# Block 3's layernorm moved to the first step of the second MLP chunk, its turning moved ahead of one weight step, and two w1 buffers exchanged

## The chip, the core and the metric

The kernel runs on one core of a Trainium2 chip. The metric is the device time of one launch in microseconds (us). The core has a matrix engine (TensorE, "PE" in the profile, with its weight loads as "PEld"), a vector engine (VectorE, "DVE"), a scalar engine (ScalarE, "ACT"), a general engine (GpSimd, "POOL") and a queue engine (SyncE, "SP"). Each takes its instructions in the order in which they were written. They wait for each other by semaphores. Transfers are issued here from SP's queue and from POOL's.

## The reference

x is 2048 rows of 640 numbers. Each row is layernormed; the result goes through a Fourier layer and through an MLP, and both are added to x:

```python
xn = _layernorm(x, axis=-1)
a = einsum("bsd,ed->bse", xn, dft_hid_re)      # wr
b = einsum("bsd,ed->bse", xn, dft_hid_im)      # wi
y = einsum("ts,bse->bte", dft_seq_re, a) - einsum("ts,bse->bte", dft_seq_im, b)
h = gelu(einsum("bsd,df->bsf", xn, w1) + b1)   # w1 is 640 x 1536
out = x + y + einsum("bsf,fd->bsd", h, w2) + b2
```

Everything is float32. A product is made of three matmuls, since each operand is split in a rounded part and a rest (`split`: ScalarE copies the rounded part, VectorE subtracts it from the source).

## The kernel before, in words

The MLP takes the 2048 rows in four chunks t of 512. The first two are done in full; the last two share products by sums and differences of operands (the letters a11, s1, ob and so on in `form_of`, and the w1 sums in `sums_w1`). After the MLP come the products of the Fourier layer, which fill the rest of the program.

The change lies in the second chunk (t = 1), in the branch `elif i < NF - 2` of the main loop. One pass of it, unit i = 0 to 9, is for the PE fifteen matmuls of `hidden(g + 2)` (the first MLP product, two units ahead, g = 12 + i) and fifteen of `output(g)` (the second). What `hidden` leaves in a PSUM bank, `gelu(g + 2)` turns into a pair `hs`: ScalarE applies gelu and copies the rounded part, VectorE subtracts the rest. `output(g)` reads the pair that was made two units before. The pairs are called here by their g: pair 18 is made in unit 4 and read in unit 6, pair 19 is made in unit 5 and read in unit 7.

Behind these, each unit writes side work to the same queues, in this order: `second_block(i)`, then `prep_w(k)` by the table `w_early`.

- Rows 12 to 15 (128 rows each) are block 3, the fourth chunk's rows in their natural order: `ln_stats`, `ln_scale` and `ln_apply` normalize them on VectorE (one square root on ScalarE), and 16 transfers, L203, write them to the DRAM tensor `xs`. `load_z(t)` reads a chunk back as the tile z, four transfers on SP, and `turn_z2` / `turn_z1` transpose z on VectorE (lines L786 and L792). z2 is the third chunk, z3 the fourth. The tile z, the tile xo and the later wz share one buffer, `zo`.
- `prep_w(0)` to `prep_w(5)` prepare two of the five column blocks j of wr and wi, three steps for each. Step 0 and 3 transpose both (L396, out of `wraw`) and issue the loads of the next block; every step splits its pieces into the staging tile `wst` and has POOL write them to the DRAM tensor `wit` (L418). The first step of a block writes two pieces, the second two, the third three. `wst` holds two of the wide pieces, so a step's ScalarE copy waits until the step before has landed in `wit`. That wait also holds up whatever ScalarE and VectorE have queued behind, the next gelu among it.
- From unit 7 on `sums_w1` and `split_w1` make the sums of w1 in a tile `rq` and split them into the tiles TW[0], TW[1], ... (pool "twp", tags tw0 and tw1). That pool takes the place of the pool of `wst`, `wraw` and `wt` when `open_tw` runs.

After unit 9 come the last two outputs, `head(0)`, `mid(0)`, `head(1)` and `finish(0)`: the products of the shared chunks. Between them stand the second chunk's five closing blocks, e = 0 to 4 (`outs`): ScalarE adds the bias in PSUM (L368), VectorE transposes the bank (L371), POOL adds it to xo (L373). `forms_ob` stands among them: one add of 1024 columns (L452), the split of TW[1], and the split of the form ob. `head(1)` starts in the bank of block e = 2, then in that of e = 3; the first product of `finish(0)` goes on in a bank that a VectorE add of `mid(0)` (L452, `banks<-banks,fifth`) reads.

No scheduler reorders this: the order in the queues is the order in which the code writes it.

Of the kernel before, what the change touches and what calls it, by code (L numbers as in the profile page):

```python
# [11 lines left out]
F32R = mybir.dt.float32r  # L12
# [3 lines left out]
P = 128  # L16
# [10 lines left out]
def kernel(  # L27
# [57 lines left out]
    def pool(name, side="left", stack=ctx):  # L85
        return stack.enter_context(tc.tile_pool(name=name, bufs=1, side=side, reuse_waits="tile"))
# [93 lines left out]
    def ln_stats(c):  # L180
        m = MV
        st = ST[c % 2]
        half = D // 2
        for h in range(2):
            nc.vector.bn_stats(st[:, h, :], xt[c][:, h * half : (h + 1) * half])
        nc.vector.bn_aggr(m[:, c % 4, 0:2], st.rearrange("p a b -> p (a b)"))
# [12 lines left out]
    def ln_apply(c, queue=nc.sync):  # L199
        m = MV[:, c % 4]  # L200
        nc.vector.tensor_scalar(xt[c], xt[c], m[:, 0:1], m[:, 3:4], op0=ALU.subtract, op1=ALU.mult)
        for k in range(NC):
            queue.dma_start(xs[c % NC * NC + k, c // NC * B : (c // NC + 1) * B], xt[c][k * B : (k + 1) * B])  # L203
# [25 lines left out]
    def load_z(t):  # L229
        z = out_pool.tile([P, NB, DQ], F32, tag="zo", bufs=1, name=f"z{t}")  # L230
        Z["z"] = z
        for q in range(Q):
            v = xs[:, t * B : (t + 1) * B, q * DQ : (q + 1) * DQ].rearrange("n r d -> r n d")
            nc.sync.dma_start(z[q * B : (q + 1) * B], v)
# [124 lines left out]
    def load_xo(t):  # L359

        xo[t] = out_pool.tile([P, NB, DQ], F32, tag="zo", bufs=1, name=f"xo{t}")
        for q in range(Q):
            nc.sync.dma_start(xo[t][q * B : (q + 1) * B], rows_of(x, t)[:, :, q * DQ : (q + 1) * DQ])
# [12 lines left out]
    A = {}  # L376
# [43 lines left out]
    def prep_w(s):  # L420

        j, k = divmod(s, 3)
        if j >= ND:
            return
        if k == 0:
            turn_w(0, j)
            turn_w(1, j)
            if j + 1 < ND and j != WEARLY - 1:
                load_w(0, j + 1)
                load_w(1, j + 1)  # L430
        (r1, r2, r4), (i1, i2, i4) = (
            (A["wt", m][:, : 2 * P], A["wt", m][:, 2 * P : 4 * P], A["wt", m][:, 4 * P :]) for m in range(2)
        )
# [12 lines left out]
        if k == 2:  # L446
            put_w(3, j, r1)
            put_w(4, j, i1)
            put_w(5, j, r2)
# [325 lines left out]
    TW, RQ = {}, {}  # L775
    parks = {}

    def form_of(name, cc, src, dst):
        FX[name, cc] = dst
        split(dst[:, 0], dst[:, 1], src)  # L780

    def lane(tag, k):
        return whole[tag][:, k * 2 * TB : (k + 1) * 2 * TB].rearrange("p (a b) -> p a b", a=2)
# [7 lines left out]
    def turn_z1(dst, j):  # L791
        nc.vector.transpose(dst.rearrange("p (n i) -> p n i", i=B), Z["z"][:, :, j * B : (j + 1) * B])  # L792

    def two(lo):
        return A["zs"][:, lo * TB : (lo + 2) * TB].rearrange("p (a b) -> p a b", a=2)

    def load_rq(q):
        if q >= NF // 2:
            return
        RQ[q] = A["xf"].tile([P, 4, 2 * P], F32, tag="rq", bufs=1, name=f"rq{q}")  # L800
        v = w1.rearrange("(q c i) f -> q i c f", q=Q, i=B)
        for k in range(Q):
            nc.sync.dma_start(RQ[q][k * B : (k + 1) * B], v[k, :, :4, 2 * q * P : 2 * (q + 1) * P])

    def sums_w1(q):
# [6 lines left out]
        add(r[:, 2:4, P:], r[:, 2:4, P:], r[:, 0:2, :P], ALU.subtract)  # L812
        add(r[:, 2:4, :P], r[:, 2:4, :P], r[:, 2:4, P:], ALU.subtract)

    def split_w1(q):
        if q >= NF // 2:
            return
        TW[q] = A["tw"].tile([P, 2, 8 * P], F32R, tag=f"tw{q % 2}", bufs=1, name=f"tw{q}")
        split(TW[q][:, 0], TW[q][:, 1], RQ.pop(q).rearrange("p a b -> p (a b)"))
        TW[q] = TW[q].rearrange("p a (c f) -> p a c f", c=4)  # L820

# [148 lines left out]
    def open_tw():  # L970
        A["es"].close()
        A["w"] = None
        A["es"] = ExitStack()
        A["tw"] = pool("twp", stack=A["es"])

    def open_xf():
        es_rows.close()
        A["esx"] = ExitStack()
        A["xf"] = pool("xfp", side="right", stack=A["esx"])
        A["xfx"] = A["xf"].tile([P, 2, 2, TB], F32R, name="xfx")  # L980
        A["fifth"] = A["xf"].tile([P, TB], F32, name="fifth")
        load_rq(0)

    def second_block(i):

        if i == 0:
            load_z(2)
            ln_stats(12)
            ln_stats(13)
        if i == 1:  # L990
            ln_stats(14)
            ln_stats(15)
        if i == 2:
            ln_scale(12, 4)
            for c in range(12, 16):
                ln_apply(c, nc.gpsimd if c < 14 else nc.sync)
        if i == 3:
            A["zs"] = place("xc01", (P, 30 * P), F32, name="zs")
            turn_z2(two(0), 0)
            turn_z2(two(2), 2)  # L1000
            turn_z1(ZT[:, 0], 4)
            load_z(3)
        if i == 4:
            form_of("a11", 0, two(0)[:, 0], lane("as", 5))
            open_xf()
        if i == 5:
            form_of("a11", 1, two(0)[:, 1], lane("xc23", 0))
            form_of("oa", 0, ZT[:, 0], lane("xc23", 1))
        if i == 6:
            form_of("a12", 0, two(2)[:, 0], lane("xc23", 2))  # L1010
            turn_z2(ZT, 2)
            turn_z2(two(4), 0)
            turn_z1(A["zs"][:, 6 * TB : 7 * TB], 4)
            load_xo(1)
            open_tw()
        if i == 7:
            sums_w1(0)
            split_w1(0)
            load_rq(1)
            form_of("a22", 0, ZT[:, 0], lane("r01", 0))  # L1020
        if i == 8:
            form_of("a22", 1, ZT[:, 1], lane("r01", 1))
            add(ZT, ZT, two(4))
        if i == 9:
            form_of("s1", 0, ZT[:, 0], lane("r01", 2))
            form_of("s1", 1, ZT[:, 1], lane("r01", 3))
            add(two(4), two(0), two(4), ALU.subtract)
            add(ZT, ZT, two(0), ALU.subtract)
# [18 lines left out]
        form_of("s4", 0, two(2)[:, 0], XTT[:, 3])  # L1047
        form_of("s4", 1, two(2)[:, 1], XTT[:, 4])

    w_early = {0: (0,), 1: (1,), 2: (2,), 3: (3,), 4: (4,), 5: (5,)}  # L1050
    prep_w1(3)
    gelu(1, acc1)
    for g in range(NG):
        t, i = divmod(g, NF)
        if t == 0:
            if i:
                prep_w1(i + 3)
            prep_w2(i + 1)
            load_w1(i + 6)
            load_w2(i + 4)  # L1060
            if i != 8:
                first_block(i)
            if i == NF - 1:
                open_w()
                acc = hidden(g + 2)
                output(g)

                def fill(k):
                    for e in ((0,), (1, 2))[k]:
                        add_block(xo[0], e, oacc[0][e], f"ot0_{e}", bias=b2c[:, e : e + 1])  # L1070

                gelu(g + 2, acc, fill)
                outs(0, (3, 4))
            elif i == NF - 2:
                output(g)
                gelu(g + 2, hidden(g + 2))
            else:
                acc = hidden(g + 2) if g else acc2
                if i == NF - 3:
                    for j in range(ND):  # L1080
                        prep_xt(1, j)
                        if j + 2 < ND:
                            transpose_z(1, j + 2)
                gelu(g + 2, acc)
                if i == 8:
                    first_block(i)
                if i == 9:
                    ln_stats(10)
                    ln_stats(11)
                output(g)  # L1090
        elif i < NF - 2:
            acc = hidden(g + 2)
            gelu(g + 2, acc)
            output(g)
            second_block(i)
            for k in w_early.get(i, ()):
                prep_w(k)
        elif i == NF - 2:
            output(g)
            forms_s2()  # L1100
            head(0)
            forms_s3()
        else:
            output(g)
# [36 lines left out]
        outs_at((3, 4), (0, 1), done=True)  # L1141

    outs(1, (0,), yt=lambda n: AB[:, 0], done=False)
    forms_ob()
    outs_at((2, 1), (4, 5))
    mid(0, rest)
    forms_s4()
    head(1)
# [657 lines left out]
```

## Time and profile before

| | us |
|---|---|
| median of 3 runs | 850.76 |
| lowest and highest | 850.23, 850.90 |
| the profiled execution's own time | 853.42 |
| its span, first to last instruction | 851.6 |
| PE busy in the span | 842.5 |
| VectorE, ScalarE, GpSimd busy | 668.0, 355.3, 53.6 |

The profile is of one execution. A row of the timeline gives the start from the beginning of the span, the duration (of all merged instructions), the engine, the line, the operation, the tiles out<-in, the shape and the count; in square brackets stands how long the engine had been idle and what ended that. A matmul of 512 columns stays in the array for 0.39 us, but the next one starts 0.227 us behind it, so PE rows overlap, and a lost moment shows as a start that comes late.

### The profile page before, as it was taken

How to read it: one execution, taken by the hardware profiler on the slowest of the kernel's cores; microseconds unless marked ns; L12 is line 12 of the kernel's file. 1: busy time of each engine (PE TensorE's matmuls, PEld its weight loads, DVE VectorE, ACT ScalarE, POOL GpSimd, SP SyncE). 2: the span in 40 equal slices, each digit the busy share in tenths (PEclk: the TensorE clock that was granted, in tenths of full speed). 3: DMA queues.
4: the chain of work that ended last, by engine and by line, in shares of the span. 5: the costliest groups of instructions: out<-in, count | busy, mean ns of one | idle time of the engine just before them, and what ended most of it. 6: DMA issues, size and time to landing. Idle time of an engine off the chain costs nothing.

```text
span 851.6 us, 10345 instructions
## 1 busy us (share of the span) xinstructions
PE 842.5 (99%) x3707; PEld 694.5 (82%) x3707; DVE 668.0 (78%) x841; ACT 355.3 (42%) x499; POOL 53.6 (6%) x78
## 2 busy tenths in 40 slices
PE   8999999999999999999999999999999999999997
PEld 6888888778888888888888888888888888888886
DVE  6766764795757888879988787899977898885687
ACT  7454533555655554333434343232322423223241
POOL 0000313131221300000000000000000000000001
PEclk9999999999999999999999999999999999999999
DMA  6667799738669998948743669763865879805464
GB/s 185 187 185 186 162 215 252 196 79 195 207 216 347 360 218 158 188 102 204 164 137 95 177 211 285 171 139 97 213 164 171 253 184 228 312 18 179 124 170 108
DMA packets 207363, 158.45 MB, mean 186 GB/s; under 512 B 81040, under 2 KB 180880, under 8 KB 206800
## 3 DMA queue, kind: packets, MB, share of 16 engines
q1 hardware_dynamic: 198368, 134.59, 62.2%
q0 software_dynamic: 4400, 21.89, 6.5%
q10 hardware_dynamic: 4544, 1.31, 0.6%
q8 instruction: 29, 0.48, 0.2%
q14 instruction: 22, 0.18, 0.1%
HBM read 114.76 MB, written 42.99 MB: 185 GB/s over the span
## 4 chain that ended last, share of the span: by engine, by line
PE 83%; DVE 4%; DMA 4%; ACT 3%; issue 3%; SPq 2%; POOL 1%; ACTq 0%; POOLq 0%; DVEq 0%
PE banks L278 27%; PE banks L279 26%; PE banks L280 26%; PE banks L304 3%; DMA x<-in_A_x_dram 1%; DMA wit<-wst 1%; SPq L388 1%; DMA xs<-x 1%; ACT ab L322 1%; SPq L203 0%; SPq L178 0%; POOL wit L418 0%; DVE r L161 0%; ACT hs L326 0%; DVE tw L161 0%
## 5 line engine op out<-in xcount | busy, mean ns | idle before, releaser
L278 PE MATMUL banks<-as,xab 128*128 128x512 f32 x411 | 160.0, 389 | 0.6 <-DVE zs L371 0.6
L279 PE MATMUL banks<-as,xab 128*128 128x512 f32 x411 | 159.9, 389 | 0.0
L280 PE MATMUL banks<-as,xab 128*128 128x512 f32 x411 | 159.9, 389 | 0.0
L160 ACT ACTIVATE as<-r 128x1024 fp32r<-128x1024 f32 x80 | 85.0, 1062 | 177.9 <-PE banks L280 149.5
L161 DVE TENSOR_TENSOR as<-r,as 128x1024 fp32r<-128x1024 f32 x80 | 97.1, 1215 | 41.5 <-ACT as L160 41.5
L278 PEld LDWEIGHTS banks<-as,xab 128*128 128x128 f32 x411 | 77.2, 188 | 17.0 <-DVE zs L371 1.0
L279 PEld LDWEIGHTS banks<-as,xab 128*128 128x128 f32 x411 | 77.2, 188 | 16.0
L280 PEld LDWEIGHTS banks<-as,xab 128*128 128x128 f32 x411 | 77.2, 188 | 15.9
L278 PE MATMUL banks<-as,xc 128*128 128x512 f32 x224 | 87.1, 389 | 0.0
L279 PE MATMUL banks<-as,xc 128*128 128x512 f32 x224 | 87.1, 389 | 0.0
L280 PE MATMUL banks<-as,xc 128*128 128x512 f32 x224 | 87.1, 389 | 0.0
L160 ACT ACTIVATE as<-rt 128x1024 fp32r<-128x1024 f32 x32 | 34.0, 1063 | 70.5 <-PE banks L280 62.5
L304 PE MATMUL banks<-xtt,xab 128*128 128x512 f32 x240 | 57.2, 391 | 0.2 <-ACT xtt L160 0.2
L304 PEld LDWEIGHTS banks<-xtt,xab 128*128 128x128 f32 x240 | 44.7, 188 | 10.1 <-ACT xtt L160 0.6
L278 PEld LDWEIGHTS banks<-as,xc 128*128 128x128 f32 x224 | 42.1, 188 | 8.8
L280 PEld LDWEIGHTS banks<-as,xc 128*128 128x128 f32 x224 | 42.1, 188 | 8.7
L279 PEld LDWEIGHTS banks<-as,xc 128*128 128x128 f32 x224 | 42.0, 188 | 8.7
L161 DVE TENSOR_TENSOR as<-rt,as 128x1024 fp32r<-128x1024 f32 x32 | 38.8, 1211 | 5.3 <-ACT as L160 5.3
L160 ACT ACTIVATE as<-u 128x1024 fp32r<-128x1024 f32 (+1 forms) x24 | 22.1, 919 | 48.2 <-PE banks L280 48.2
L512 DVE STREAM_TRANSPOSE r<-raw 128x1024 f32<-128x1024 f32 x32 | 39.5, 1239 | 3.0 <-PE banks L280 2.4
L161 DVE TENSOR_TENSOR as<-u,as 128x1024 fp32r<-128x1024 f32 (+1 forms) x24 | 24.9, 1041 | 18.8 <-ACT as L160 18.8
L512 DVE STREAM_TRANSPOSE rt<-raw 128x1024 f32<-128x1024 f32 x32 | 38.8, 1229 | 0.9 <-PE banks L280 0.8
(353 smaller groups left out, 1622.9 us busy)
## 6 DMA issues: line engine op xcount, KB each, us to landing
raw<-in_A_dft_seq_re_dram SPq DMA_DIRECT2D x64, 256.0 KB, 5.5
raw<-in_A_dft_seq_im_dram SPq DMA_DIRECT2D x64, 256.0 KB, 5.1
ws<-wit SPq DMA_DIRECT2D x15, 384.0 KB, 5.8
xo<-in_A_x_dram SPq DMA_DIRECT2D x16, 320.0 KB, 5.9
xab<-wit SPq DMA_DIRECT2D x13, 384.0 KB, 4.0
wit<-wstp POOLq DMA_DIRECT2D x12, 384.0 KB, 3.7
x<-in_A_x_dram SPq DMA_DIRECT2D x14, 320.0 KB, 4.4
xs<-x SPq DMA_DIRECT2D x56, 80.0 KB, 1.8
```

The lines of the kernel that those rows point to most:

```text
L160: nc.scalar.activation(h, s, AF.Copy)
L161: nc.vector.tensor_tensor(l, s, h.bitcast(F32), op=ALU.subtract)
L278: nc.tensor.matmul(acc, wh, mh, start=first, stop=False, skip_group_check=goes_on)
L279: nc.tensor.matmul(acc, wh, ml, start=False, stop=False, skip_group_check=goes_on)
L280: nc.tensor.matmul(acc, wl, mh, start=False, stop=last, skip_group_check=goes_on)
L304: nc.tensor.matmul(acc, W1[i][:, a, j * P : (j + 1) * P], XT[j][:, b], start=n == 0, stop=n == len(steps) - 1)
L322: nc.scalar.activation(a, acc, AF.Gelu_apprx_tanh, bias=b1c[:, i : i + 1])
L388: nc.sync.dma_start(t[q * B : (q + 1) * B], v[:, :, s0 : s0 + B])
L512: nc.vector.transpose(held(pieces[g][2], u).rearrange("p c (n i) -> p c n i", i=B), r.rearrange("p n (c i) -> p c n i", i=B))
```

## The change

Six edits, all in the order of the side work:

1. `ln_stats`, `ln_scale` and `ln_apply` of rows 12 to 15 are all written in unit 0, ahead of `prep_w(0)`, instead of in units 0, 1 and 2. The writes of rows 12 and 13 thereby stand ahead of all of `prep_w` in POOL's queue, and those of rows 14 and 15 ahead of `load_z(2)` in SP's.
2. `prep_w(3)`, `(4)` and `(5)` move from units 3, 4, 5 to units 4, 5, 6.
3. z3 is turned in unit 5, behind the forms of that unit and ahead of `prep_w(4)`, instead of in unit 6 behind `prep_w(5)`. `load_xo(1)`, which needs z3's buffer, moves with it.
4. `load_rq(0)` is written in unit 5 instead of unit 4.
5. TW[1] is allocated at `open_tw`, ahead of TW[0], so that TW[0] gets the upper and TW[1] the lower place, the one in which `wst` lay.
6. Of the closing blocks, e = 2 is written ahead of `forms_ob`, and e = 1 stays behind it.

```diff
     def split_w1(q):
         if q >= NF // 2:
             return
-        TW[q] = A["tw"].tile([P, 2, 8 * P], F32R, tag=f"tw{q % 2}", bufs=1, name=f"tw{q}")
+        if q != 1:
+            new_tw(q)
...
         A["tw"] = pool("twp", stack=A["es"])
+        new_tw(1)
...
         A["fifth"] = A["xf"].tile([P, TB], F32, name="fifth")
-        load_rq(0)
...
         if i == 0:
-            load_z(2)
-            ln_stats(12)
-            ln_stats(13)
-        if i == 1:
-            ln_stats(14)
-            ln_stats(15)
-        if i == 2:
+            for c in range(12, 16):
+                ln_stats(c)
             ln_scale(12, 4)
             for c in range(12, 16):
                 ln_apply(c, nc.gpsimd if c < 14 else nc.sync)
+            load_z(2)
...
-        if i == 6:
-            form_of("a12", 0, two(2)[:, 0], lane("xc23", 2))
             turn_z2(ZT, 2)
             turn_z2(two(4), 0)
             turn_z1(A["zs"][:, 6 * TB : 7 * TB], 4)
+            load_rq(0)
             load_xo(1)
+        if i == 6:
+            form_of("a12", 0, two(2)[:, 0], lane("xc23", 2))
+            prep_w(5)
             open_tw()
...
-    w_early = {0: (0,), 1: (1,), 2: (2,), 3: (3,), 4: (4,), 5: (5,)}
+    w_early = {0: 0, 1: 1, 2: 2, 4: 3, 5: 4}
...
     outs(1, (0,), yt=lambda n: AB[:, 0], done=False)
+    outs_at((2,), (4,))
     forms_ob()
-    outs_at((2, 1), (4, 5))
+    outs_at((1,), (5,))
```

VectorE around z3. In the names, `hs` is a gelu pair, `wst<-wt_1` a split of the second column block of wr (1217, 1258) or wi (1219, 1260), `zt/zs<-z_1212` the turning of z3, `xc<-zs` and `xc<-zt` the splits of forms. Before, from pair 19 on:

```order
L328 TENSOR_TENSOR hs<-ab,hs 128x512
L161 TENSOR_TENSOR xc_127<-zs,xc_127 128x512
L161 TENSOR_TENSOR xc_127<-zt,xc_127 128x512
L161 TENSOR_TENSOR wst<-wt_1_1217,wst 128x256
L161 TENSOR_TENSOR wst<-wt_1_1219,wst 128x256
L161 TENSOR_TENSOR wst<-wt_1_1217,wst 128x256
L328 TENSOR_TENSOR hs<-ab,hs 128x512
L161 TENSOR_TENSOR xc_127<-zs,xc_127 128x512
L786 STREAM_TRANSPOSE zt<-z_1212 128x1024
L786 STREAM_TRANSPOSE zs<-z_1212 128x1024
L792 STREAM_TRANSPOSE zs<-z_1212 128x512
L328 TENSOR_TENSOR hs<-ab,hs 128x512
```

and now, from pair 19 on as well:

```order
L328 TENSOR_TENSOR hs<-ab,hs 128x512
L161 TENSOR_TENSOR xc_127<-zs,xc_127 128x512
L161 TENSOR_TENSOR xc_127<-zt,xc_127 128x512
L786 STREAM_TRANSPOSE zt<-z_1212 128x1024
L786 STREAM_TRANSPOSE zs<-z_1212 128x1024
L792 STREAM_TRANSPOSE zs<-z_1212 128x512
L161 TENSOR_TENSOR wst<-wt_1_1260,wst 128x256
L417 SCALAR_TENSOR_TENSOR wst<-wt_1_1260,wst 128x128
L452 TENSOR_TENSOR wt_1_1260<-wt_1_1260,wt_1_1258 128x256
L161 TENSOR_TENSOR wst<-wt_1_1260,wst 128x256
```

Behind pair 19 stood the last step of the block; now the turning of z3 stands there, and then the block's middle step, so two steps of wr and wi come behind it.

SP's queue in the same units. `wraw0_1` and `wraw1_1` are the loads of the second column block, `xs<-x14, x15` the writes of block 3's rows, `ys` the stores that free the buffer `zo` for z2. Before:

```order
L930 DMA ys2_62<-xo0_842 2048x1x32
L234 DMA z2_1018<-xs_59 32x16x160 x4
L388 DMA wraw0_1_1033<-in_A_dft_hid_re_dram 32x20x32 x4
L388 DMA wraw1_1_1038<-in_A_dft_hid_im_dram 32x20x32 x4
L203 DMA xs_59<-x14_877 32x640 x4
L203 DMA xs_59<-x15_879 32x640 x4
L234 DMA z3_1212<-xs_59 32x16x160 x4
L803 DMA rq0_1273<-in_B_w1_dram 32x4x256 x4
L363 DMA xo1_1376<-in_A_x_dram 32x16x160 x4
```

and now:

```order
L934 DMA ys2_62<-xo0_842 2048x1x32
L203 DMA xs_59<-x14_877 32x640 x4
L203 DMA xs_59<-x15_879 32x640 x4
L234 DMA z2_1056<-xs_59 32x16x160 x4
L388 DMA wraw0_1_1065<-in_A_dft_hid_re_dram 32x20x32 x4
L388 DMA wraw1_1_1070<-in_A_dft_hid_im_dram 32x20x32 x4
L234 DMA z3_1212<-xs_59 32x16x160 x4
L803 DMA rq0_1313<-in_B_w1_dram 32x4x256 x4
L363 DMA xo1_1318<-in_A_x_dram 32x16x160 x4
```

The row writes moved from behind the second block's loads to ahead of z2; z3 now follows those loads directly.

POOL's queue at the start of the chunk, as a difference (`wit` are the writes of the staged pieces):

```order
+L203 DMA xs<-x_873 32x640 x4
+L203 DMA xs<-x_875 32x640 x4
 L418 DMA wit_63<-wst 128x768
 L418 DMA wit_64<-wst 128x768
 L418 DMA wit_69<-wst 128x768
 L418 DMA wit_65<-wst 128x768
-L203 DMA xs<-x_873 32x640 x4
-L203 DMA xs<-x_875 32x640 x4
```

The eight writes of rows 12 and 13 moved from behind the first four staged writes to ahead of them.

More of the change, by code (lines that the diff above doesn't have):

```diff
@@ L813, in sums_w1, with new_tw @@
         add(r[:, 2:4, :P], r[:, 2:4, :P], r[:, 2:4, P:], ALU.subtract)
+    def new_tw(q):
+        TW[q] = A["tw"].tile([P, 2, 8 * P], F32R, tag=f"tw{q % 2}", bufs=1, name=f"tw{q}")
     def split_w1(q):
@@ L1095 @@
             second_block(i)
-            for k in w_early.get(i, ()):
-                prep_w(k)
+            if i in w_early:
+                prep_w(w_early[i])
         elif i == NF - 2:
```

## Prediction

> **What bounds the kernel now.** I read the page first, then PE's rows stretch by stretch, then the rows of the engines that ended its gaps.
>
> ```profile
> PE 842.5 (99%) x3707; PEld 694.5 (82%) x3707; DVE 668.0 (78%) x841; ACT 355.3 (42%) x499; POOL 53.6 (6%) x78
> ```
>
> PE is busy for 842.5 of 851.6 us, so only what stands between its matmuls can be won. Next, the stretches around the change: length, PE's busy time, matmuls. The first three run from one `hidden` to the next, units 6, 7 and 8; the last is from the last three matmuls of `mid(0)` to the end of `mid(1)`.
>
> ```profile
> 139.70:146.87 7.17, 7.13 (x31) 1.00 0.65 179
> 146.87:155.21 8.34, 7.36 (x31) 1.00 1.01 275
> 155.21:162.01 6.80, 6.80 (x31) 1.00 0.29 117
> 182.41:196.66 14.25, 13.67 (x58) 10.47 (x57) 9.41 (x14) 4.86 (x9) 5.50 (x4) 1.00 0.67 148
> ```
>
> An undisturbed unit takes 6.80 us, 30 steps of 0.2267. Unit 6 takes 0.37 more, unit 7 takes 1.54 more. The last stretch holds 57 steps (the three that end `mid(0)`, `head(1)` 12, `finish(0)` 21, `mid(1)` 21), 12.92 us, and takes 14.25: 1.33 more. Together 3.24 us. The rows that start late:
>
> ```profile
> 143.52 0.50 PE L279 MATMUL banks<-hs,r 128*128 128x512 f32 x1
> 150.83 0.49 PE L278 MATMUL banks<-hs,r 128*128 128x512 f32 x1 [0.39 <-ACT hs L326]
> 151.91 0.50 PE L279 MATMUL banks<-hs,r 128*128 128x512 f32 x1 [0.58 <-DVE hs L328]
> 183.83 0.50 PE L278 MATMUL banks<-as,xab 128*128 128x512 f32 x1 [0.58 <-DVE zs L371]
> 186.82 0.50 PE L278 MATMUL banks<-r,tw 128*128 128x512 f32 x1
> ```
>
> The first three are `output` waiting for pairs 18 and 19. The fourth is `head(1)`, which waits for the turning of block e = 2. The fifth is `finish(0)`: fifteen steps behind 182.41 it would start at 185.81, so 1.01 us are lost by then, and it starts just behind VectorE's add of the banks (below). The other 0.32 of the 1.33 lie behind it.
>
> Now the engines behind them, mostly VectorE; ScalarE, POOL and SP by name.
>
> ```profile
> 102.41 2.38 SPq L178 DMA_DIRECT2D x<-in_A_x_dram  x4
> 112.25 0.85 DVE L396 STREAM_TRANSPOSE wt<-wraw 128x640 f32<-128x640 f32 x1 [4.30 <-DMA wraw<-in_A_dft_hid_re_dram]
> 114.80 0.84 DVE L396 STREAM_TRANSPOSE wt<-wraw 128x640 f32<-128x640 f32 x1 [1.71 <-DMA wraw<-in_A_dft_hid_im_dram]
> 116.46 1.32 POOL L418 DMA_DIRECT2D wit<-wst  x2 [11.80 <-DVE wst L161]
> 126.16 2.18 DVE L201 TENSOR_SCALAR x<-x,mv 128x640 f32<-128x640 f32 x4
> 127.07 4.30 POOL L203 DMA_DIRECT2D xs<-x  x8 [3.32 <-DVE x L201]
> 130.89 1.28 ACT L322 ACT_TABLE_LOAD   x1
> 133.57 0.69 DVE L328 TENSOR_TENSOR hs<-ab,hs 128x512 fp32r<-128x512 f32 x1 [2.24 <-ACT hs L326]
> 140.00 0.84 DVE L396 STREAM_TRANSPOSE wt<-wraw 128x640 f32<-128x640 f32 x1 [2.14 <-DMA xs<-x]
> 142.78 0.69 DVE L328 TENSOR_TENSOR hs<-ab,hs 128x512 fp32r<-128x512 f32 x1 [0.61 <-ACT hs L326]
> 147.16 0.43 DVE L161 TENSOR_TENSOR wst<-wt,wst 128x256 fp32r<-128x256 f32 x1 [3.10 <-ACT wst L160]
> 149.37 0.63 DVE L161 TENSOR_TENSOR wst<-wt,wst 128x256 fp32r<-128x256 f32 x2 [1.24 <-ACT wst L160]
> 151.16 0.68 DVE L328 TENSOR_TENSOR hs<-ab,hs 128x512 fp32r<-128x512 f32 x1
> 150.29 0.54 POOL L418 DMA_DIRECT2D wit<-wst  x1 [1.66 <-DVE wst L161]
> 154.70 1.26 ACT L160 ACTIVATE wst<-wt 128x256 fp32r<-128x256 f32 x3 [2.89 <-DMA wit<-wst]
> 157.24 0.69 DVE L328 TENSOR_TENSOR hs<-ab,hs 128x512 fp32r<-128x512 f32 x1 [0.82 <-ACT hs L326]
> 158.45 1.24 DVE L786 STREAM_TRANSPOSE zt<-z 128x1024 f32<-128x1024 f32 x1
> 160.74 0.67 DVE L792 STREAM_TRANSPOSE zs<-z 128x512 f32<-128x512 f32 x1
> 161.90 1.60 DVE L452 TENSOR_TENSOR rq<-rq 128x512 f32<-128x512 f32 x3
> 163.54 1.06 ACT L160 ACTIVATE tw<-rq 128x1024 fp32r<-128x1024 f32 x1 [4.56 <-DVE rq L452]
> 164.63 1.23 DVE L161 TENSOR_TENSOR tw<-rq,tw 128x1024 fp32r<-128x1024 f32 x1 [1.13 <-ACT tw L160]
> 179.35 2.12 POOL L373 TENSOR_TENSOR xo<-xo,ab 128x512 f32<-128x512 f32 x1 [21.88 <-DVE ab L371]
> 180.24 2.31 DVE L161 TENSOR_TENSOR tw<-rq,tw 128x1024 fp32r<-128x1024 f32 x1
> 185.50 1.26 DVE L452 TENSOR_TENSOR banks<-banks,fifth 128x512 f32<-128x512 f32 x2
> ```
>
> Pair 18 ends at 143.47, behind step 3 of wr and wi, which could not start before 140.00; pair 19 ends at 151.84, behind step 4, whose pieces waited for staged writes. From 164.63 VectorE works nearly without a gap up to 186.76, the add that `finish(0)` waits for. That second chain matters most below.
>
> **The change, part by part.**
>
> Edit 1, rows in the wait. VectorE idles 4.30 us ahead of 112.25 and 1.71 ahead of 114.80. The last x load is issued at about 104.5; at 4.5 us to land (row below) and two halves of statistics, scaling can begin at about 111, and root, scale and the four applications (2.18) end at about 114.4. The two transposes then run to 116.0, 0.3 us later than now: the cover holds. The square root's table load and the one back (1.28 each) move off the way of pair 17 to that of pair 15: behind the transposes come copies (0.6), the load (1.28) and the pair (2.0), so it ends at 119.9; it is needed at 122.70, four units ahead of 149.90, where pair 19 would be needed without the waits. POOL issues eight row writes (4.30 us) from about 112.8 on, so its first staged write goes out at 117.1, 0.65 later. These writes and SP's eight now share the engines with `ys` and the staged writes, which delays z2 by 0.5 to 1.6 us; the same work is then missing at 127 to 141, where the second block loads. I take the two as equal and let that block arrive at 140.0 again.
>
> Edit 2, a unit later. Pair 18 has only z2's turning in front. Pair 17 ends now at 134.26; without the table load and with later writes I leave it there; 2.95 us of turning and 0.6 for the pair give 137.8, needed at 143.10. Pair 19 takes the place that pair 18 has now, 143.5, needed at 149.90. Both are over 5 us early, so the 0.37 and 1.54 go: minus 1.91.
>
> Edit 3, z3 first. This is what is late next. z3 may load when z2 is turned, at 137.2, and its four issues end at 139.0 (a row has 2.81 us for them now). How long they take to land, how long the fourth staged write (row 150.29) takes, the same write of the first block (issued at 123.21, right behind z2's loads), all of the chunk's staged writes, and x:
>
> ```profile
> 141.63 2.81 SPq L234 DMA_DIRECT2D z<-xs  x4
> DMA to landing us min/median/max: 4.2/6.9/8.7
> DMA to landing us min/median/max: 5.2/5.2/5.2
> DMA to landing us min/median/max: 7.2/7.2/7.2
> DMA to landing us min/median/max: 2.3/4.0/7.2
> x<-in_A_x_dram SPq DMA_DIRECT2D x4, 320.0 KB, 4.5
> ```
>
> z3: the last issue at 139.0 plus 8.7 is 147.7 (plus 6.9, 145.9; and 149.0 if wr and wi, ahead in the queue, hold it up longer). I take 147.7, because the last of four ran to the maximum both times. VectorE has pair 19 and two forms behind it by 145, waits 2.7 us and turns z3 until 150.7 (2.95, from 158.45 to 161.41). Then step 4: first piece and sum, 1.0 us (147.16 to 148.1), ScalarE's copy, VectorE's rest and POOL's issue, 1.4 (148.9 to 150.29): the fourth staged write goes out at 153.1 instead of 150.29. Pair 20 ends near 154.9, needed at 156.7: covered, with 1.8 us.
>
> Step 5 copies its third piece when that write has landed. I take 5.2 us (the same transfer) and keep 4.0 and 7.2 as ends: 158.3, and the copy (0.42) ends at 158.7, against 155.96 now. From there to the end of TW[0]'s split, from the rows: pair 21 1.97 (155.96 to 157.93, though that is pair 20 now), sums 1.60, copy 1.06, rest 1.23, 5.86 together: 164.6. Now it ends at 165.86, since z3's turning stands in between. So the chain behind is 1.3 us earlier. Pair 21 ends at 160.7, needed at 163.5; pair 22 ends 1.3 behind TW[0], 165.9, needed at 166.9.
>
> Edit 6, e = 2 first. The bank of `head(1)` is free 4 us earlier, so the wait at 183.83 goes by itself. But the same instructions stand between 164.63 and the add at 185.50, none removed, so `finish(0)` still waits for that add: now 186.82, then 1.3 earlier. Against it, POOL's add for e = 2 now falls beside `forms_ob`. The split at 180.24 took 2.31 us beside one such add, the same shape at 164.63 took 1.23 alone. A second one costs between 0 and 1.08; I take 0.5, half, since part of it can run beside a transpose. `finish(0)` starts at 186.0: minus 0.8.
>
> By the Trainium skill, SBUF — State Buffer, section SBUF: two separate sides, VectorE with two SBUF inputs and a GpSimd operation hold a shared pair of ports exclusively, for the whole instruction. By that rule the second add costs its full 1.08, and the sum would be minus 0.2 instead of minus 0.8; if they only shared bandwidth, less than half. The trace agrees with the rule in the one place that it shows.
>
> Edits 4 and 5. rq0 lands near 150 and is read at 160.7; TW[0]'s new place was last read by VectorE itself, so it waits for no staged write; TW[1]'s place waits for the last three, 15 us earlier. All at nothing; without edit 5 the split of TW[0] would wait for a write issued near 159, some 3 us.
>
> **Sum.** PE by itself would reach `finish(0)` 1.91 + 1.01 = 2.92 us earlier; VectorE lets it 0.8 us earlier. The 0.32 behind it stay, as that start is late again. Minus 0.8 us: the span goes from 851.6 to 850.8, the profiled execution from 853.42 to 852.6; the median, 2.66 below that execution, from 850.76 to 850.0. That is minus 0.1%, and 0.2% (1.7 us) is about what a measurement tells from no change.
>
> **Rivals.** First, VectorE finds z3 in place. Each us that z3 or the staged write comes earlier is one us off the chain, until PE's own 2.92 is reached. With z3 at 146.5 and the write in 4.0 us, `finish(0)` starts 2.4 earlier than forecast and all of 2.92 goes, perhaps the 0.32 too: 847.5 to 847.8, and up to 849.0 for less of it. For it: a median of 4.0 for the writes, and the 16 row writes are gone from 127 to 141. Against it: in SP's queue z3 stands directly behind the loads of wr and wi.
>
> Second, slower: xo1's loads, now issued when z3 is turned, at 150.7, stand right ahead of the fourth staged write, as z2's did ahead of the one that took 7.2. With that, 2.0 us more, and z3 at 149.0, 1.3 more, `finish(0)` starts 2.5 us later than now and pair 22 is late too: 853.3. It decides from a landing of the fourth staged write at 160.8, where the loss passes 1.7 us. For it: by the program z2 and xo1 move the same number of bytes in pieces of the same length. Against it: it needs both delays.
>
> By the Trainium skill, DMA: Bandwidth & Descriptors, section Queues, rings and completion order, each DMA engine goes round robin between queues that have work, packet by packet. By that rule POOL's write would get every other turn beside xo1, and would land nearer to 4.0 than to 7.2, 1.2 us better than the sum. The trace does not bear it out beside z2, where 7.2 were needed.
>
> Third, the rows don't fit into the wait: if x lands 3 us later than its median, the transposes at 112.25 and 114.80 move by as much and pairs 15 to 17 with them; pair 17, needed at 136.30, has 2 us of room. Less than 1 us lost, inside the forecast's own range.
>
> **Chances.** Within 0.2%: 0.50, with its own range 849.1 to 852.4. Faster, the first rival: 0.34. Slower, the second: 0.16. The range 847.6 to 852.8 takes in the first rival but for its end (0.05 left out) and the second up to both delays at three quarters (0.13 left out).
>
> **What would show it.** Right: units 6 and 7 at 6.80 us each; VectorE without a long idle time ahead of the first transpose of wr; z3's turning between pair 19 and step 4 with an idle time of 1 to 4 us ahead of it; `finish(0)` just behind a VectorE add of the banks, at 185 to 187. Wrong: no wait at `finish(0)` (first rival), a late `output` in units 5, 9 or 10, or a landing of the fourth staged write behind 160.8 (second).

## The result and the profile after

| | before | after |
|---|---|---|
| median (us) | 850.73 | 855.61 |
| lowest and highest | 850.23, 851.91 | 854.61, 858.31 |
| runs | 6 | 6 |
| the profiled execution's own time | 853.42 | 855.73 |
| its span | 851.6 | 854.0 |

The change makes the kernel slower: 1.0064 times the time before, 95% interval 1.0046 to 1.0081, that is 4.9 us by the medians. The two profiled executions differ by 2.3 us only. The profile of before fell on an execution that took 2.7 us more than the median of its kernel; the one of after took 0.1 us more. The traces can therefore explain 2.3 us directly, and the other 2.6 us are a fact about the profile of before, which the first experiment is about.

PE's busy time on the page of after:

```profile
PE 842.2 (99%) x3707; PEld 693.9 (81%) x3707; DVE 668.5 (78%) x841; ACT 355.4 (42%) x499; POOL 53.8 (6%) x78
```

It is 842.5 before: the matmuls are the same, and what was lost stands between them. The windows view of after, on the same matmuls as the prediction's table: units 6, 7 and 8, and the 57 steps from the last three matmuls of `mid(0)` to the end of `mid(1)`:

```profile
139.88:146.68 6.80, 6.80 (x31) 5.63 (x30) 5.29 (x12) 3.49 (x8) 1.08 (x2) 1.00 1.01 199
146.68:153.48 6.80, 6.80 (x31) 5.63 (x30) 4.42 (x8) 1.23 (x5) 0.54 (x1) 1.00 0.80 223
153.48:160.28 6.80, 6.80 (x31) 5.63 (x30) 3.28 (x8) 2.46 (x6) 0.54 (x1) 1.00 1.08 289
183.09:198.82 15.73, 13.54 (x59) 10.54 (x58) 10.41 (x14) 5.75 (x11) 5.55 (x4) 1.00 0.63 136
```

Units 6 and 7 take 6.80 us each, where they took 7.17 and 8.34. The last stretch takes 15.73 instead of 14.25. PE's rows of after that start late:

```profile
167.96 0.50 PE L278 MATMUL banks<-hs,rt 128*128 128x512 f32 x1 [0.72 <-ACT hs L326]
168.69 0.50 PE L279 MATMUL banks<-hs,rt 128*128 128x512 f32 x1 [0.22 <-DVE hs L328]
182.28 0.50 PE L278 MATMUL banks<-xtt,tw 128*128 128x512 f32 x1 [0.56 <-ACT banks L861]
187.39 0.50 PE L278 MATMUL banks<-r,tw 128*128 128x512 f32 x1 [2.06 <-DVE zs L371]
189.18 0.51 PE L278 MATMUL banks<-r,tw 128*128 128x512 f32 x1
```

The first two are `output(22)`, waiting for pair 22: 1.5 us that were not there before. The third is `mid(0)`, waiting for a bank that ScalarE copies (0.72). The fourth is the second bank of `head(1)`, e = 3: it waits for VectorE's turning and starts 2.45 us behind the row ahead of it (184.94), 2.22 more than a step. The fifth is `finish(0)`. It starts at 189.18 against 186.82, 2.36 us later, and that is the whole difference of the two spans.

The rows behind these starts, of VectorE, ScalarE, SP and POOL (a line "DMA to landing" gives the time from issue to landing, here for the last two of xo1's loads and then for the fourth staged write):

```profile
114.46 1.57 DVE L396 STREAM_TRANSPOSE wt<-wraw 128x640 f32<-128x640 f32 x2
136.56 2.37 DVE L786 STREAM_TRANSPOSE zs<-z 128x1024 f32<-128x1024 f32 x2 [2.81 <-DMA z<-xs]
142.35 0.84 DVE L396 STREAM_TRANSPOSE wt<-wraw 128x640 f32<-128x640 f32 x1 [0.89 <-DMA wraw<-in_A_dft_hid_im_dram]
148.75 1.25 DVE L786 STREAM_TRANSPOSE zt<-z 128x1024 f32<-128x1024 f32 x1 [1.74 <-DMA z<-xs]
152.63 1.02 SPq L363 DMA_DIRECT2D xo<-in_A_x_dram  x2
DMA to landing us min/median/max: 5.9/6.8/7.8
154.24 0.54 POOL L418 DMA_DIRECT2D wit<-wst  x1 [0.91 <-DVE wst L161]
DMA to landing us min/median/max: 6.9/6.9/6.9
161.16 0.42 ACT L160 ACTIVATE wst<-wt 128x256 fp32r<-128x256 f32 x1 [1.18 <-DMA wit<-wst]
166.19 1.23 DVE L161 TENSOR_TENSOR tw<-rq,tw 128x1024 fp32r<-128x1024 f32 x1 [1.13 <-ACT tw L160]
180.90 1.28 POOL L373 TENSOR_TENSOR xo<-xo,ab 128x512 f32<-128x512 f32 x1 [17.89 <-DVE ab L371]
181.29 1.98 DVE L452 TENSOR_TENSOR zs<-zs,zt 128x1024 f32<-128x1024 f32 x1
187.86 1.26 DVE L452 TENSOR_TENSOR banks<-banks,fifth 128x512 f32<-128x512 f32 x2
```

The rows of block 3 fit into the wait: the transposes of wr and wi are done at 116.03. z2 has become late (136.56, with 2.81 us of idling ahead of it), and the second block's wi too (142.35). z3 is turned from 148.75 on. Then the last of xo1's loads goes out at 153.16 (152.63 and 0.53 behind it) and lands at 160.96; the fourth staged write goes out behind it, at 154.24, and lands at 161.13. ScalarE's copy of step 5's third piece starts at 161.16, where it was 155.54 before. TW[0]'s split ends at 167.42 instead of 165.86, 1.56 us later. Between that and `finish(0)`, which starts behind the add of the banks at 187.86, another 0.80 us are lost: what the add at 181.29 takes more than before (1.98 against 1.18).

### The profile page after: what moved, and what is told of

It is laid out like the page before. It is cut to its first block, busy times and chain, and to the rows that moved or that the text cites. A ratio compares the mean times of both kernels' runs of the same rounds, so it can differ in the third digit from the quotient of the medians.

```text
span 854.0 us, 10344 instructions
## 1 busy us (share of the span) xinstructions
PE 842.2 (99%) x3707; PEld 693.9 (81%) x3707; DVE 668.5 (78%) x841; ACT 355.4 (42%) x499; POOL 53.8 (6%) x78
## 4 chain that ended last, share of the span: by engine, by line
PE 82%; issue 5%; DVE 4%; DMA 4%; ACT 2%; SPq 1%; POOL 1%; ACTq 0%; DVEq 0%; POOLq 0%
PE banks L278 26%; PE banks L279 26%; PE banks L280 26%; PE banks L304 3%; DMA x<-in_A_x_dram 2%; DMA wit<-wst 1%; DMA xs<-x 1%; POOL wit L418 0%; SPq L203 0%; ACT ab L322 0%; DVE xtt L161 0%; DVE r L161 0%; SPq L256 0%; SPq L178 0%; DVE zs L452 0%
```

## The experiments

All ratios are to the kernel before on the same chip, with 95% intervals.

**The kernel before, profiled once more.** Nothing is edited.

> The kernel before, profiled once more. The execution that the prediction was worked out from took 853.42 us, and the other runs of the same kernel 850.2 to 851.9. Theory A (the profiled execution had stalls that most runs do not have): the span comes out at 848.5 to 849.5, and of the 3.24 us of stalls in units 6 and 7 and around head(1) and finish(0), 2 to 2.7 us are missing, those of units 6 and 7 (1.91) first. Theory B (the stalls are in every run and profiling adds 2.7 us elsewhere): the same 3.24 us are there again.

Median 850.43 us (11 runs), ratio 0.9998 (0.9990 to 1.0007). The profiled execution took 852.66 us, again the slowest of them, and the other ten 849.93 to 852.07. SP, POOL, its landing, and PE, in this trace:

```profile
140.95 2.97 SPq L234 DMA_DIRECT2D z<-xs  x4
140.96 1.14 POOL L418 DMA_DIRECT2D wit<-wst  x2 [7.04 <-DVE wst L161]
DMA to landing us min/median/max: 5.1/5.1/5.1
151.31 0.50 PE L279 MATMUL banks<-hs,r 128*128 128x512 f32 x1 [0.58 <-DVE hs L328]
```

Neither theory is right as it stood: unit 6 has lost its 0.37, but `output(19)` still waits 1.35 us in all, and the span is 850.9. The rows show what decides it. Step 3's staged writes and z3's loads go out at the same moment (140.96 and 140.95; 141.65 and 141.63 in the first trace), and the first write lands 5.1 us later, at 146.06, behind the first of z3's four loads (145.19) and ahead of the second (147.38). A third trace of the same code up to unit 9 is that of the experiment with edit 6 alone, below. There the writes won, at 140.17 against z3's 140.99:

```profile
140.99 2.50 SPq L234 DMA_DIRECT2D z<-xs  x4
140.17 1.14 POOL L418 DMA_DIRECT2D wit<-wst  x2 [5.84 <-DVE wst L161]
DMA to landing us min/median/max: 2.9/2.9/2.9
```

That write landed in 2.9 us, and units 6 and 7 both took 6.80 us. So the stalls of units 6 and 7 in the kernel before are 1.91, 1.35 or 0, by which of two queues is first by less than 1 us. Most runs of before, with spans of 848.2 to 849.5 in all but one, are 1.4 to 3.4 us below the two profiled ones. The third kind alone is not enough for that: its trace spans 850.7 us, and without the 0.80 that edit 6 costs there (below) it would span some 849.9, an estimate from the two numbers. Waits of `head(1)` and `finish(0)` would have to be missing from most of those runs too. They have no trace, so this is not shown.

**xo1's loads a unit later.**

```diff
             load_rq(0)
-            load_xo(1)
...
             prep_w(5)
+            load_xo(1)
             open_tw()
```

> The changed kernel with load_xo(1) back behind prep_w(5) in unit 6. Theory X (xo1's loads, issued just ahead of it, hold up the fourth staged write): the write issued at about 154.2 lands in 4 to 5.2 us instead of 6.9, pair 22 is in time (the 1.5 us of waiting at 168 to 169 go) and finish(0) starts 1.7 to 2.4 us earlier; the time is 853 to 854. Rival Z (the write is slow whatever stands beside it, or the lateness is z3's): the landing stays at 6 to 7 us, and the time stays at 855 to 856.

856.15 us, ratio 1.0061 (1.0049 to 1.0073): no change. But the edit moved nothing on the chip. SP's and ScalarE's rows:

```profile
151.40 1.91 SPq L363 DMA_DIRECT2D xo<-in_A_x_dram  x4
160.92 0.42 ACT L160 ACTIVATE wst<-wt 128x256 fp32r<-128x256 f32 x1 [1.36 <-DMA wit<-wst]
```

`prep_w(5)` gives SP no instruction, so the loads follow rq0 in its queue wherever they are written, and go out as soon as z3 is turned. The staged write landed in 6.9 us, as before. So this run does not tell the theories apart.

**Edit 6 undone in the changed kernel.**

```diff
-    outs_at((2,), (4,))
     forms_ob()
-    outs_at((1,), (5,))
+    outs_at((2, 1), (4, 5))
```

> The changed kernel with edit 6 undone: e = 2 and e = 1 both behind forms_ob. Theory P (a second GpSimd add beside forms_ob holds VectorE's instructions up): the last add of 1024 columns in forms_ob goes back from 1.98 to about 1.2 us, finish(0) starts 0.8 us earlier, and the wait of mid(0) for ScalarE's bank copy (0.72) goes; the time is 854.5 to 855.1. Rival Q (the order costs nothing, the chain only comes late from the staged write): 855.5, and head(1) waits instead for its bank, as before.

855.22 us, ratio 1.0051 (1.0039 to 1.0063); the interval overlaps that of the changed kernel. In the trace VectorE's add is back at 1.18 us and `finish(0)` starts at 188.11, 1.07 us earlier than with edit 6, of which 0.25 had been there ahead of `forms_ob` already (its turning of e = 0 starts at 179.81 against 180.06):

```profile
180.45 1.18 DVE L452 TENSOR_TENSOR zs<-zs,zt 128x1024 f32<-128x1024 f32 x1
182.03 0.50 PE L278 MATMUL banks<-xtt,tw 128*128 128x512 f32 x1 [0.61 <-ACT banks L861]
185.13 0.50 PE L278 MATMUL banks<-as,xab 128*128 128x512 f32 x1 [1.44 <-DVE zs L371]
```

Theory P is right on the add and wrong on `mid(0)`: its wait at 182.03 is still there (0.77 against 0.72), so it comes from the chain being late and not from edit 6. `head(1)` waits for its first bank now (1.61) instead of its second (2.22): edit 6 had only moved that wait.

**Edit 1 undone in the changed kernel.** Statistics and writes of rows 12 to 15 in units 0, 1 and 2 again, `load_z(2)` ahead of them.

```diff
         if i == 0:
+            load_z(2)
+            ln_stats(12)
+            ln_stats(13)
+        if i == 1:
+            ln_stats(14)
+            ln_stats(15)
+        if i == 2:
-            for c in range(12, 16):
-                ln_stats(c)
             ln_scale(12, 4)
...
-            load_z(2)
```

> The changed kernel with edit 1 undone: statistics and writes of rows 12 to 15 in units 0, 1 and 2, and z2's loads ahead of them. Theory R (the row writes ahead of z2 delay z2, then the second block of wr and wi, then z3): z2 lands about 4 us earlier, step 3's first transpose comes at 138 to 140 instead of 140.6, z3 lands 0.5 to 2 us earlier than 148.6, and the time is 853.5 to 855. Rival S (the two delays are equal, as the prediction took it): z3 lands at 148 to 149 in both, and the time stays at 855.2 to 856.

858.94 us, ratio 1.0097 (1.0082 to 1.0112): slower by another 3.3 us. VectorE's first turning of z3:

```profile
151.69 1.25 DVE L786 STREAM_TRANSPOSE zt<-z 128x1024 f32<-128x1024 f32 x1 [7.39 <-DMA z<-xs]
```

Both theories miss. z3 waits for the row writes and is turned 2.94 us later (151.69 against 148.75), with 7.39 us of idling ahead. Given edits 2 and 3, which need z3 early, edit 1 is the one that helps.

**xo1's loads behind load_rq(1).** That load waits for the split of TW[0], so SP cannot pass it.

```diff
             load_rq(0)
-            load_xo(1)
...
             load_rq(1)
+            load_xo(1)
```

> The changed kernel with load_xo(1) written behind load_rq(1) in unit 7. In the earlier try, behind prep_w(5) in unit 6, the four loads were still issued at 151.4 to 152.8, since nothing stands between them and rq0 in SP's queue; load_rq(1) waits for the split of TW[0], so now they go out behind 167. Theory X (xo1's loads hold the staged writes up): the two writes of step 4 land within 2.3 to 3 us instead of 6.4 and 6.9, step 5's pieces are copied by 157.5 instead of 161.2, the 1.5 us at output(22) go, finish(0) starts 1.5 to 3.5 us earlier; the time is 851.5 to 853.5. Rival Z (the write is slow by itself, or z3's landing at 148.6 decides): landings of 6 to 7 us stay, 855 to 856.

851.51 us, ratio 1.0009 (1.0000 to 1.0018): 4.1 us of the 4.9 are gone. SP, POOL and its landing, ScalarE and PE:

```profile
165.47 3.38 SPq L363 DMA_DIRECT2D xo<-in_A_x_dram  x4
154.81 0.54 POOL L418 DMA_DIRECT2D wit<-wst  x1 [0.90 <-DVE wst L161]
DMA to landing us min/median/max: 2.6/2.6/2.6
157.40 0.42 ACT L160 ACTIVATE wst<-wt 128x256 fp32r<-128x256 f32 x1 [0.64 <-DMA wit<-wst]
183.83 0.50 PE L278 MATMUL banks<-r,tw 128*128 128x512 f32 x1 [0.21 <-DVE zs L371]
```

xo1 goes out at 165.47. The same staged write, issued 0.6 us later than in the changed kernel, lands in 2.6 us instead of 6.9. Step 5's third piece is copied at 157.40 instead of 161.16, `output(22)` waits for nothing, and `finish(0)` starts at 185.62, 3.56 us earlier. Theory X holds: xo1's loads, which edit 3 brought ahead of the staged writes, are most of the loss. The rival Z falls, since z3 was turned even later here (149.60) than in the changed kernel.

**The same, with edit 6 undone too.** Both diffs above together.

> The same with edit 6 undone as well. Theory P (the second GpSimd add and the order of ScalarE's bank adds cost by themselves): another 0.4 to 1.2 us less than with xo1 behind rq1 alone, 850 to 852.5, and the last 1024-column add of forms_ob at about 1.2 us. Rival Q (edit 6 only shows where the chain is late already): no difference between the two, within 0.3 us.

851.10 us, ratio 1.0006 (0.9997 to 1.0014). The difference of 0.4 us to the run above lies inside both intervals. The profiled execution took 850.39 us with a span of 848.6, and no row of PE between 130 and 195 us has a wait in it.

**Edit 1 alone in the kernel before.** The edit of `second_block(0)` to `(2)` in the change's diff, and nothing else of it.

> The kernel before with edit 1 alone. Undoing edit 1 in the changed kernel made it 3.3 us slower, so there the early rows are a gain. Theory G (a gain by itself, since z3 and the second block no longer wait for the row writes): z3 lands at 147 to 149 instead of 151.2, the staged writes behind it land 2 to 3 us earlier, and the stalls of units 6 and 7 shrink; 849 to 850.2. Rival H (z2, some 4 us later, makes step 3 and pair 18 late and takes it back): output(18) waits 1 to 2 us; 850.5 to 852.5.

857.43 us, ratio 1.0082 (1.0068 to 1.0097): 6.9 us slower, more than any theory gave it. SP, POOL, the landing of its two writes, and PE:

```profile
139.36 1.90 SPq L234 DMA_DIRECT2D z<-xs  x4
143.11 1.14 POOL L418 DMA_DIRECT2D wit<-wst  x2 [10.22 <-DVE wst L161]
DMA to landing us min/median/max: 7.8/7.9/8.0
154.35 0.73 PE L278 MATMUL banks<-hs,r 128*128 128x512 f32 x1 [2.47 <-ACT hs L326]
```

Two things happen. z2 is late, so step 3 is late and `output(18)` waits 1.8 us. And z3 no longer waits for the rows, so all its loads and three of rq0's four stand ahead of step 3's writes (139.36 to 142.69, against 143.11), which now take 7.8 to 8.0 us; step 4, pair 19 and `output(19)` (over 4 us) wait for them. z3 itself is not turned until 159.29 in this kernel: its loads came early for nobody, at the cost of writes that were awaited.

**Edit 6 alone in the kernel before.**

```diff
+    outs_at((2,), (4,))
     forms_ob()
-    outs_at((2, 1), (4, 5))
+    outs_at((1,), (5,))
```

> The kernel before with edit 6 alone. Theory P (second GpSimd add beside forms_ob, and ScalarE's bank add ahead of the copy that mid(0) waits for): the last 1024-column add of forms_ob goes from 1.18 to about 2.0 us, finish(0) starts 0.8 us later, mid(0) waits some 0.7; 851 to 851.8. Rival Q (the bank of head(1) comes free earlier and nothing else changes): head(1)'s wait of 0.7 goes, 849.8 to 850.5.

851.59 us, ratio 1.0011 (1.0002 to 1.0020). VectorE's add, and the second bank of `head(1)`:

```profile
178.37 1.98 DVE L452 TENSOR_TENSOR zs<-zs,zt 128x1024 f32<-128x1024 f32 x1
184.48 0.50 PE L278 MATMUL banks<-r,tw 128*128 128x512 f32 x1 [1.68 <-DVE zs L371]
```

The add takes 1.98 us again. The wait for the first bank of `head(1)` is gone, and the second bank waits 1.84 us in its place. No wait of `mid(0)` shows. By itself edit 6 costs 0.2 to 1.7 us.

**z3 and rq0 behind step 3's writes, on POOL's queue.** To see whether it is the order of issue that counts, and not the queue, the kernel before with edit 1 issues them there:

```diff
-            nc.sync.dma_start(z[q * B : (q + 1) * B], v)
+            eng.dma_start(z[q * B : (q + 1) * B], v)
...
-            nc.sync.dma_start(RQ[q][k * B : (k + 1) * B], v[k, :, :4, 2 * q * P : 2 * (q + 1) * P])
+            (nc.sync if q else nc.gpsimd).dma_start(RQ[q][k * B : (k + 1) * B], v[k, :, :4, 2 * q * P : 2 * (q + 1) * P])
...
-            load_z(3)
...
             for k in w_early.get(i, ()):
                 prep_w(k)
+            if i == 3:
+                load_z(3, nc.gpsimd)
```

> The kernel before with edit 1, and the loads of z3 and rq0 issued on POOL's queue behind step 3's two staged writes instead of on SP's. Theory F (a staged write lands only when the loads issued ahead of it have landed, whatever their queue): step 3's writes, now ahead of z3, land within 4 us of issue (by 147) instead of 7.8 (150.9 and 151.7), so the 4.2 us at output(19) go; the 1.8 us at output(18), which come from z2 being late, stay: 852 to 854. Rival W (the writes are slow because GpSimd's queue is served after SP's, or the lateness is z2's alone): 856 to 858.

856.69 us, ratio 1.0069 (1.0056 to 1.0081). POOL's rows, the landings of step 3's and of step 4's two writes, and PE:

```profile
143.97 1.14 POOL L418 DMA_DIRECT2D wit<-wst  x2 [12.56 <-DVE wst L161]
DMA to landing us min/median/max: 2.6/2.9/3.2
145.50 2.61 POOL L234 DMA_DIRECT2D z<-xs  x4 [0.38 <-issue]
148.10 2.19 POOL L803 DMA_DIRECT2D rq<-in_B_w_dram  x4
DMA to landing us min/median/max: 5.9/6.2/6.5
160.73 0.50 PE L278 MATMUL banks<-hs,r 128*128 128x512 f32 x1 [1.23 <-ACT hs L326]
```

The mechanism of theory F holds and its time does not. Step 3's writes, now ahead of z3, land in 2.6 to 3.2 us instead of 7.8 to 8.0, and `output(19)` waits no longer. But step 4's writes now stand behind z3 and rq0 and take 5.9 to 6.5, so step 5 and pair 20 are late instead: 2.0 us at `output(20)`, from 160.73 on. `output(18)` still waits for step 3, now 2.4 us where it was 1.8. The loads have only been moved from ahead of one awaited write to ahead of the next.

**The same, with z2's loads ahead of the row writes on SP.**

```diff
         if i == 0:
+            load_z(2)
             for c in range(12, 16):
                 ln_stats(c)
...
-            load_z(2)
```

> The same, with z2's loads ahead of the writes of rows 14 and 15 in SP's queue. Theory F with the place of z2 as the second half of edit 1's cost: z2 lands 3 to 4 us earlier (132 to 133), the 1.8 us at output(18) go as well, and with no wait of output left the time is 849.5 to 851. Rival W: z2 is late through the row writes on the DMA engines themselves, wherever it stands; output(18) still waits over 1 us, 852 to 854.

856.56 us, ratio 1.0072 (1.0058 to 1.0086): nothing gained. SP and PE:

```profile
123.78 1.91 SPq L234 DMA_DIRECT2D z<-xs  x4
126.11 6.91 SPq L203 DMA_DIRECT2D xs<-x  x8
133.11 2.41 SPq L388 DMA_DIRECT2D wraw<-in_A_dft_hid_re_dram  x4
136.84 0.50 PE L278 MATMUL banks<-hs,xc 128*128 128x512 f32 x1 [0.28 <-ACT hs L326]
145.15 0.51 PE L278 MATMUL banks<-hs,r 128*128 128x512 f32 x1 [0.72 <-ACT hs L326]
```

z2 goes out 2.6 us earlier (it was 126.35), but the rows behind it push the second block's loads to 133.11 (from 129.78), and the staged writes of step 2 as well. So `output(17)` waits now (1.05), and `output(18)` (1.5) and `output(20)` (1.7) still do. Rival W is nearer. The transfers are the same in both orders, and each order made another of them late.

**z3 and rq0 on POOL's queue in the kernel before, rows where they were.** The diff of the POOL experiment without edit 1.

> The kernel before, rows where they were, with the loads of z3 and rq0 on POOL's queue behind step 3's writes. Theory F: those writes land within 4 us (144 to 145) instead of 5.1 and 6.7, and the waits of output(18) and (19) that the profiled executions of before show go; the profiled execution is 1 to 1.9 us below 852.7, and the median, in whose runs these waits seem to be absent, stays within 0.6 us: 849.9 to 850.6. Rival W: nothing moves, profiled 852.7 to 853.4 and median 850.5.

852.17 us, ratio 1.0018 (1.0008 to 1.0027), slower, which neither theory gave. In the trace step 3's writes land in 2.6 to 3.1 us and units 6 and 7 take 6.80, as theory F has it; step 4's second write takes 6.2, and the profiled execution (852.3) is 0.4 and 1.1 below the two of before. Less than the 1.35 to 1.91 is won, since `head(1)` now waits 1.41 us for VectorE where it waited 0.74 and 0.80. The median has risen all the same. It fits that most runs of before have no stalls there to lose, while the late fourth write is new to them, but without their traces this is argued and not shown.

**xo1 behind rq1, edit 6 undone, z2 first.** The three diffs together, on the changed kernel.

> The changed kernel with xo1 behind rq1, edit 6 undone, and z2's loads ahead of the row writes on SP. Theory E (with xo1 out of the way the second chunk has slack, PE is the bound, and no order of the side work gives more): 850.4 to 851.2, within 0.5 us of the same without z2 first (851.1), with no wait of output in the trace. Rival V (the earlier z2 and z3 carry through VectorE's chain to finish(0)): 849 to 850.2, which would beat both kernels.

851.06 us, ratio 1.0007 (0.9998 to 1.0016), as without z2 first: theory E. No wait of PE between 130 and 190 us is left in this trace either. Where PE is free of waits, as in these two traces, the order of that side work has nothing left to win. No variant beat the kernel before.

## Why the prediction was wrong

The prediction said 850.0 us and no measurable change; it became 855.6. Of the 5.6 us, 3.1 are the chain (2.3 slower between the two profiled executions, where 0.8 faster was said), and 2.5 the base. The 3.1 come together at `finish(0)`, said for 186.0 and measured at 189.18: the fourth staged write went out 1.1 us later than said, landed after 1.7 us more than said, and VectorE's add cost 0.3 more than said. Point by point:

- **The two stalls of units 6 and 7 go.** Right in the trace: 6.80 us each. Pairs 18 and 19 ended at 140.1 and 145.8 where 137.8 and 143.5 were said, still early enough.
- **The median, 2.66 below that execution.** Wrong: these are the 2.5 us. This step carried the distance of one execution to the median over unchanged, and took the stalls of that execution as those of every run. The profiled execution of after is only 0.1 us above its median. Two further traces of the same code show 1.35 and 0 us in units 6 and 7 instead of 1.91, by a race of two queues. That is a part of the 2.5; what the rest is stays open. The table of times had spoken against this step: a profiled execution 2.5 us above the highest run leaves little of 3.24 us of stalls in the others.
- **Edit 1, the rows in the wait.** The VectorE side was right: the transposes ended at 116.03 (116.0 predicted). "I take the two as equal" was wrong: z2 was turned from 136.56 on, where 134.18 had been the start before, and the second block's wi came at 142.35 where 140.0 was said for the block. What it is worth hangs on the other edits: 3.3 us gained in the changed kernel, 6.9 lost in the kernel before.
- **Edit 3, z3 first.** z3 was turned until 151.7, where 150.7 was said, inside the given ends. The fourth staged write went out at 154.24, 1.1 later than said.
- **The landing of the fourth staged write, 5.2 us.** This is the step that failed in the chain. It took 6.9, and at 1.7 of the 3.1 us it is the largest part. Nor was 5.2 the write's own time: in the kernel before it stood behind rq0's loads, the last of which was issued at 146.23 and landed at 154.01, and the write landed at 155.52. The sum carried that wait over as if it belonged to the write, into a kernel in which other loads stand ahead of it. The prediction had kept 7.2 as an end, and had written the cause down as its second rival: xo1's loads right ahead of the write. It gave the rival 0.16, since it "needs both delays". But the delay of the write was no matter of chance: xo1 waits for z3's buffer, and step 4 for VectorE's turning of z3, so the loads go out just ahead of the writes whenever z3 comes, and the landings behind them were 6.9, 6.9 and 7.6 us in three kernels. Pair 22 was late with it, at 168.6 instead of 165.9. The rival's price was 2.5 us at `finish(0)`, and the trace shows 2.36; its deciding point was a landing at 160.8, and it was 161.13. Moving xo1 away took the landing to 2.6 us and the time to 851.5.
- **The rule that spoke for the forecast.** By the Trainium skill, DMA: Bandwidth & Descriptors, section Queues, rings and completion order, an engine takes turns between queues, so the write should have landed nearer to 4.0. The runs do not bear that out: 6.9 behind xo1, and 2.6 without it.
- **A second POOL add costs 0.5.** It costs 0.80 in the traces with edit 6 (1.98 or 1.99 against 1.18). The row ahead of it shows why: POOL's add of e = 0 runs from 180.90 to 182.18; VectorE's add starts at 181.29, and 0.89 us of waiting plus 1.18 would end at 183.36; it ends at 183.27. So the one waits for the other almost in full. By the Trainium skill, SBUF — State Buffer, section SBUF: two separate sides, the first of the two holds the shared ports for its whole instruction; this trace agrees.
- **The wait at 183.83 goes by itself.** It was replaced. The bank of e = 3, the next one that `head(1)` needs, was still behind `forms_ob` and its split; the wait moved there and grew to 2.22 us. The step had counted the first of the two banks only.
- **Edits 2, 4 and 5 at nothing.** No wait in the trace of after speaks against it; they were not tried by themselves.

By the medians, xo1's place accounts for 4.1 of the 4.9 us; with edit 6 undone as well, 0.6 us or none is left. In the traces xo1's place is 3.56 us at `finish(0)`.

## What to carry to other kernels

When a load is moved to the moment when a buffer comes free, ask which awaited write goes out right behind it: in these runs the write landed behind the load, on whichever queue it was, and that was dearer than all that the move had won. A transfer that is needed late belongs behind something that is late; moving its line in the code does nothing if its own queue has nothing in between. And before a stall of a trace is counted as winnable, compare that execution's time with the other runs: what they don't have can't be won.

## What the runs showed of the hardware

Transfers issued on two queues landed here almost in the order of their issue. In each row the write is POOL's (step 4's second) and the loads are SP's four of xo1:

| kernel | last load issued, landed | write issued, landed | us |
|---|---|---|---|
| after | 153.16, 160.96 | 154.24, 161.13 | 6.9 |
| xo1 in unit 6 | 152.81, 160.2 | 154.00, 160.9 | 6.9 |
| edit 1 undone | 156.11, 164.1 | 156.91, 164.5 | 7.6 |
| xo1 behind rq1 | none ahead | 154.81, 157.4 | 2.6 |

The write lands 0.2 to 0.7 us behind the load that was issued ahead of it, and in 2.6 us where none is. Most of the delay comes before a write moves anything. In after, step 4's first staged write goes out at 152.79, the first packet of POOL's queue starts at 156.35, 3.6 us later, and the write lands after 6.4 us. With xo1 behind rq1 it goes out at 153.37, the first packet starts at 154.49, after 1.1 us, and it lands after 2.6 us. So 2.5 of the 3.8 us are a wait for a start.

With the loads and writes in one queue (z3 and rq0 on POOL) step 4's writes took 5.9 to 6.5 us, about as long. In the kernel before, less than 1 us between two queues so decides on up to 1.9 us of PE's time: in three traces of the same code z3 was level with the write twice (1.91 and 1.35 us lost) and behind it once (none lost).

What stays open: why the profiled executions of the kernel before were slower than nearly all its other runs (853.42 and 852.66 against medians of 850.4 to 850.8) while those of the variants were not, and why the variant without a wait of PE in its trace (850.39 us) has a median of 851.1. How much edits 2, 4 and 5 are worth was not measured.
